# Reordering the first loads and the first key transposes of a fused attention and two-MLP kernel on one Trainium2 core

## The chip, the cores and the metric

The kernel runs on one core of one Trainium2 chip. The metric is the device time of one execution in microseconds (us); lower is better. The stretches looked at here are the first 20 us of some 456 us.

## What is computed

The reference is softcapped attention over 2 batches, 12 heads, 448 tokens and a head width of 64, followed by two dense blocks on the 896 by 768 result:

```python
scores = scale * np.matmul(q, k.transpose(0, 1, 3, 2))
scores = cap * np.tanh(scores / cap)
attn = np.exp(scores - max); attn = attn / (attn.sum(-1) + 1e-09)
x = attn @ v
h = x @ w_in;  x = (s * relu(h) ** 2 + b) @ w_out
h = x @ w2_in; y = layernorm(h * softmax(h)) * g_ln;  out = y @ w2_out
```

The scalar `cap` is an input that lies in memory. It matters twice: the queries are multiplied by 1/(8 cap), and the kernel has two arms, of which it takes one by comparing `cap` with 32.

## The kernel before, in words

Two heads form a pair, and there are 12 pairs. A product of two float32 matrices is made of three products of a high and a low part, so queries and keys are turned on TensorE into PSUM and then split: a high part (`qh`, `kh`) is copied out, a low part (`ql`, `kl`) is the rest. The 448 keys of a head lie in four chunks; each partition of the four-key half holds four keys, each of the three-key half three. So the keys of a head are loaded in two pieces, of 64 KB (four keys to a partition) and of 48 KB (three), and the fourth chunk of a pair has keys only from the two 64 KB pieces; the rest of it is filled with zeros by GpSimd (`zero_by_key`, lines 91 to 97). The scores of a pair come as the fourth chunk (index 3, three products over all 128 rows) and the chunks 0, 1 and 2 (three terms each, two heads side by side). Each chunk goes through tanh on ScalarE.

The prologue (lines 138 to 199) runs before the branch between the two arms. There the loads of the first two pairs are issued: queries by `load_one` (line 132, 112 KB for a head), keys by `load_by_key` (line 99). SP, ScalarE and GpSimd each issue loads, in the order of the program. `cap` is loaded first on ScalarE's queue (line 143, 4 bytes); VectorE makes a row of 128 copies of its absolute value (`cap_row`, line 179), TensorE turns this into a column (`spread`, line 186), and VectorE makes `a_t`, `r_t` and `sc_t` of it (lines 190 to 194). Around the turning TensorE makes products of ones that nobody reads (`idle`): seven ahead of it (line 184) and nine behind it (line 189), all held in this order. Then every engine reads `cap_row` into a register (line 199) and takes the branch (line 1437).

In the arm taken here, `prep_first` (line 472) turns the first pair: `turn("q")`, then `turn("k")`, all four key chunks into one bank, then the copies and rests of lines 505 to 511. A helper `then` (line 882) keeps the steps in the written order on each of TensorE, VectorE, ScalarE and GpSimd. The first steps behind it (lines 950 to 960) are, in this order, two of the three products of chunk 3 of pair 0, the turning of pair 1's queries, the last product of chunk 3, the splitting of pair 1's queries on VectorE, the chunks 0 and 1 of pair 0, the turning and splitting of pair 1's keys, and chunk 2 of pair 0.

Of the kernel before, what the change touches and what calls it, by code (L numbers as in the profile page):

```python
# [10 lines left out]
F32 = mybir.dt.float32  # L11
# [4 lines left out]
ALU = mybir.AluOpType  # L16
# [4 lines left out]
def full(ap):  # L21

    return ap.bitcast(F32)
# [14 lines left out]
def tile_softcap_attention__relu2__solu(  # L38
# [15 lines left out]
    nc = tc.nc  # L54
    B, H, S, D = q.shape
# [3 lines left out]
    P = 128  # L59
    NC = 4  # L60
    CP = S // NC
# [26 lines left out]
    cap_t = cst.tile([1, 1], F32, name="cap_t")  # L88
    cap_row = cst.tile([1, P], F32, name="cap_row")

    def zero_by_key(t, by_pair):
        for par in range(2):
            threes = (slice(D, P), slice(0, D))[par]
            if by_pair:
                nc.gpsimd.memset(t[threes, :, 3:, par], 0.0)
            else:
                nc.gpsimd.memset(t[threes, par::2, 3 * D:], 0.0)

    def load_by_key(t, src, b, heads, by_pair=False, odd=None):

        n_heads = heads.stop - heads.start
        for par in range(2):
            fours, threes = (slice(0, D), slice(D, P))[::1 - 2 * par]
            lo = 4 * D if par == 0 else 3 * D
            toks = (slice(0, lo), slice(lo, S))[::1 - 2 * par]
            queue = odd if odd and par else nc.sync
            for rows, tok, n in ((fours, toks[0], 4), (threes, toks[1], 3)):
                part = src[b, heads.start + par:heads.stop:2, tok]  # L110
                if by_pair:
                    for pr in range(n_heads // 2):
                        queue.dma_start(
                            out=t[rows, pr, :n, par],
                            in_=part[pr].rearrange("(p c) d -> p c d", c=n),
                        )
                else:
                    nc.sync.dma_start(
                        out=t[rows, par:n_heads:2, :n * D],
                        in_=part.rearrange("h (p c) d -> p h (c d)", c=n),  # L120
                    )
# [10 lines left out]
    def load_one(t, src, b, pr, j, eng):  # L132
        eng.dma_start(
            out=t[:, pr, :, j],
            in_=src[b, 2 * pr + j].rearrange("(p c) d -> p c d", c=NC),
        )

    first = {}
    for raw, nm, rows in ((raws[0], "k", P), (raws[1], "q", CP)):
        first[nm] = raw.bitcast(F32)[:rows, :4 * NC * D].rearrange(  # L140
            "p (n c h d) -> p n c h d", n=2, c=NC, h=2
        )
    nc.scalar.dma_start(out=cap_t, in_=cap.partition_broadcast(1))
    load_one(first["q"], q, 0, 0, 0, nc.gpsimd)
    load_one(first["q"], q, 0, 0, 1, nc.sync)

    def last_of(engine):
        return [ins for ins in nc.cur_bb.bb.instructions if ins.engine == engine.engine][-1]

    ident = cst.tile([P, P], F32, name="ident")  # L150
    with tc.issue_after(last_of(nc.gpsimd)):
        make_identity(nc, ident)
    with tc.issue_after(last_of(nc.gpsimd)):
        for j in range(2):
            load_one(first["q"], q, 0, 1, j, nc.gpsimd)
    for pr in range(2):
        pair = slice(2 * pr, 2 * pr + 2)
        odd = nc.scalar if pr == 0 else nc.sync
        with tc.issue_after(last_of(nc.sync)):
            load_by_key(first["k"][:, pr:pr + 1], k, 0, pair, by_pair=True, odd=odd)  # L160
    with tc.issue_after(last_of(nc.gpsimd)):
        zero_by_key(first["k"], True)
    s_t = cst.tile([P, 1], F32, name="s_t")
    b_t = cst.tile([P, 1], F32, name="b_t")
    a_t = cst.tile([P, 1], F32, name="a_t")
# [1 line left out]
    sc_t = cst.tile([P, 1], F32, name="sc_t")  # L167
# [8 lines left out]
    with psum("ps_w", 1) as ps_w:  # L176
# [3 lines left out]
            out=cap_row.bitcast(U32), in0=cap_t.bitcast(U32).to_broadcast([1, P]),  # L180
# [12 lines left out]
        out=sc_t, in0=r_t, scalar1=1.0 / float(D) ** 0.5, scalar2=None, op0=ALU.mult  # L193
# [7 lines left out]
    def layers(ctx, general):  # L201
# [220 lines left out]
        ps_s = att.enter_context(psum("ps_s", 2))  # L422
        ps_t = att.enter_context(psum("ps_t", 3 if general else 1))
# [6 lines left out]
        nat = {}  # L430
# [39 lines left out]
        st = {}  # L470

        def prep_first():
            turned, parts = {}, {}
            a, b = slice(3 * P, 4 * P), slice(0, 3 * P)

            def turn(nm):
                rows = P if nm == "k" else CP
                t = nat[nm, 0]
                pool, tag = (ps_t, "t") if nm == "k" else (ps_o, "o")
                ps = pool.tile([P, 512], F32, tag=tag, name=f"p{nm}0")  # L480
                for c in range(NC):
                    nc.tensor.transpose(
                        ps[:, c * rows:(c + 1) * rows],
                        t[:rows, 0, c].rearrange("p h d -> p (h d)"), ident[:rows, :rows],
                    )
                turned[nm] = ps[:, :4 * rows]
                parts[nm] = split[nm, 0] = tuple(
                    ap_.tile([P, 4 * rows], F32R, tag=f"{nm}{x}", name=f"{nm}{x}0", bufs=3)
                    for x in "hl"
                )  # L490

            def rest(nm, cols):
                hi, lo = (x[:, cols] for x in parts[nm])
                if nm == "q":
                    nc.vector.scalar_tensor_tensor(
                        out=lo, in0=turned[nm][:, cols], scalar=sc_t, in1=full(hi),
                        op0=ALU.mult, op1=ALU.subtract,
                    )
                else:
                    nc.vector.tensor_tensor(  # L500
                        out=lo, in0=turned[nm][:, cols], in1=full(hi), op=ALU.subtract
                    )

            then(turn, "q")
            then(lambda: nc.scalar.mul(out=parts["q"][0], in_=turned["q"], mul=sc_t))
            then(turn, "k")
            then(lambda: nc.vector.tensor_copy(parts["k"][0][:, a], turned["k"][:, a]))
            then(rest, "k", a)
            then(lambda: nc.scalar.copy(out=parts["k"][0][:, b], in_=turned["k"][:, b]))
            then(rest, "q", slice(0, 4 * CP))  # L510
            then(rest, "k", b)

        def turn(nm, n):
            g, pr = divmod(n, 2)
# [38 lines left out]
        turned = {}  # L553
# [233 lines left out]
        for kk in range(KD):  # L787
            for n in range(2):
                f = slice(n * HALF, (n + 1) * HALF)
# [92 lines left out]
        def then(step, *args):  # L882
            with ExitStack() as behind:
                for ins in last.values():
                    behind.enter_context(tc.issue_after(ins))
                n = len(traced)
                step(*args)
            for ins in traced[n:]:
                if ins.engine in ordered:
                    last[ins.engine] = ins  # L890
# [41 lines left out]
        else:  # L932
# [14 lines left out]
            DEFER = NPAIR  # L947

            weights.fine = True
            then(scores_by_key, 0, 3, (0, 1))  # L950
            then(turn, "q", 1)
            then(scores_by_key, 0, 3, (2,))
            then(high, "q", 1, nc.vector)
            then(low, "q", 1)
            then(scores_by_key, 0, 0)
            then(scores_by_key, 0, 1)
            then(turn, "k", 1)
            then(high, "k", 1, nc.vector)
# [470 lines left out]
        rows = {}  # L1429
# [46 lines left out]
```

## Time and profile before

| | us |
|---|---|
| median of 3 runs | 458.34 (457.85 to 458.5) |
| the profiled execution | 458.0 |
| its span, first to last instruction | 456.2 |
| TensorE busy in the span | 450.2 |

The rows below come from the profiled execution. Times start at its first instruction. PE is TensorE's products, PEld its weight loads, DVE is VectorE, ACT ScalarE, POOL GpSimd, SP SyncE; a q behind an engine's name means its sequencer, which issues loads and waits.

### The profile page before, as it was taken

The numbers are of one execution on the slowest core, as the hardware profiler recorded it, in microseconds if no ns is written. First come the engines' busy times: TensorE is split into PE (matmuls) and PEld (weight loads), VectorE is DVE, ScalarE is ACT, GpSimd is POOL, SyncE is SP. The second block draws the span as 40 slices with busy tenths as digits, with TensorE's granted clock in tenths as the row PEclk, the third lists the DMA queues.
The fourth block names the chain that finished last, engine by engine and source line by source line (L and its number), as shares of the span: only waits on it lengthen the run. The fifth ranks groups of instructions, "written<-read, shape, count | busy, mean of one in ns | idle before, by whom it ended". The sixth has DMA issues, their size and how long they took to land.

```text
span 456.2 us, 6615 instructions
## 1 busy us (share of the span) xinstructions
PE 450.2 (99%) x2387; PEld 369.7 (81%) x2387; DVE 382.6 (84%) x634; ACT 295.4 (65%) x438; POOL 91.7 (20%) x89
## 2 busy tenths in 40 slices
PE   8999999999999999999999999999999999999996
PEld 6645455557989898988888998898988888899995
DVE  4898989868898999995699989988898999976572
ACT  4998999982776677664677755455555785873040
POOL 8178786778000000000000000000001100200000
PEclk9999999999999999999999999999999999999999
DMA  6766570014446667441323234434312230002122
GB/s 153 159 163 142 121 186 16 15 56 147 153 129 220 199 215 225 143 130 56 92 85 101 93 93 133 141 105 168 102 45 74 75 128 1 1 6 65 36 70 72
DMA packets 44742, 49.23 MB, mean 108 GB/s; under 512 B 21442, under 2 KB 37058, under 8 KB 44706
## 3 DMA queue, kind: packets, MB, share of 16 engines
q1 hardware_dynamic: 43808, 47.80, 35.9%
q0 software_dynamic: 368, 0.81, 0.7%
q8 instruction: 20, 0.33, 0.3%
q10 hardware_dynamic: 530, 0.16, 0.1%
q14 instruction: 16, 0.13, 0.1%
HBM read 46.01 MB, written 2.75 MB: 107 GB/s over the span
## 4 chain that ended last, share of the span: by engine, by line
PE 98%; DVE 0%; issue 0%
PE in L380 9%; PE y L380 9%; PE y L381 9%; PE y L382 9%; PE in L382 9%; PE in L381 9%; PE o L632 8%; PE s L590 7%; PE h L380 4%; PE h L382 4%; PE h L381 4%; PE m L642 2%; PE pk L520 1%; PE x L1254 1%; PE pq L520 1%; PE oz L381 1%
## 5 line engine op out<-in xcount | busy, mean ns | idle before, releaser
L380 PE MATMUL in<-x,h_wi 128*128 128x384 f32 (+2 forms) x192 | 70.0, 365 | 0.0
L382 PE MATMUL in<-x,l_wi 128*128 128x384 f32 (+2 forms) x192 | 69.8, 365 | 0.0
L381 PE MATMUL in<-x,h_wi 128*128 128x384 f32 (+2 forms) x192 | 69.7, 364 | 0.0
L1216 POOL TENSOR_SCALAR small<-small 128x1 f32<-128x1 f32 x7 | 3.2, 451 | 281.5 <-ACT e L1215 281.5
L412 ACT ACTIVATE gh<-g,s_t 128x384 fp32r<-128x384 f32 (+1 forms) x64 | 41.9, 667 | 13.0 <-PE y L382 12.5
L413 DVE SCALAR_TENSOR_TENSOR gl<-g,s_t,gh 128x384 fp32r<-128x384 f32 (+1 forms) x64 | 42.7, 679 | 2.9 <-ACT gh L412 2.5
L597 ACT ACTIVATE e<-s 128x896 f32<-128x896 f32 (+1 forms) x48 | 37.9, 820 | 6.1 <-PE s L590 5.7
L604 ACT ACTIVATE e<-e,a_t 128x2240 f32<-128x2240 f32 (+1 forms) x24 | 40.5, 1690 | 0.4
L380 PEld LDWEIGHTS in<-x,h_wi 128*128 128x128 f32 x192 | 36.1, 188 | 5.5 <-ACT e L604 0.7
L381 PEld LDWEIGHTS in<-x,h_wi 128*128 128x128 f32 x192 | 36.0, 188 | 3.8
L382 PEld LDWEIGHTS in<-x,l_wi 128*128 128x128 f32 x192 | 36.0, 188 | 3.7
L632 PE MATMUL o<-e,vn 128*64 128x448 f32 x192 | 38.9, 545 | 0.0
L380 PE MATMUL h<-w2i_h,y 128*128 128x512 f32 x84 | 33.1, 394 | 0.0
L382 PE MATMUL h<-w2i_h,y 128*128 128x512 f32 x84 | 33.0, 392 | 0.0
L381 PE MATMUL h<-w2i_l,y 128*128 128x512 f32 x84 | 32.6, 389 | 0.0
L632 PEld LDWEIGHTS o<-e,vn 128*64 128x64 f32 x192 | 13.7, 136 | 19.6 <-issue 15.7
L615 POOL TENSOR_TENSOR c<-c,e 128x896 f32<-128x896 f32 x11 | 24.1, 2190 | 15.5 <-DVE c L621 11.9
L252 ACT ACTIVATE wt_wi<-raw 128x768 f32<-128x768 f32 x15 | 13.4, 903 | 20.4 <-DVE l_wi L277 10.2
L612 POOL TENSOR_TENSOR c<-e 128x896 f32<-128x896 f32 x11 | 23.2, 2111 | 11.5 <-ACT e L604 11.3
L590 PE MATMUL s<-qh,kh 64*128 64x448 f32 (+1 forms) x84 | 21.2, 436 | 0.0
L590 PEld LDWEIGHTS s<-qh,kh 64*128 64x128 f32 (+1 forms) x84 | 9.0, 184 | 12.2 <-issue 11.5
L274 ACT CAST h_wi<-wt_wi 128x768 fp32r<-128x768 f32 x16 | 13.3, 828 | 8.7 <-DVE wt_wi L268 7.3
(595 smaller groups left out, 1210.9 us busy)
## 6 DMA issues: line engine op xcount, KB each, us to landing
raw<-in_moe_w_in_dram SPq DMA_DIRECT2D x16, 768.0 KB, 4.8
raw<-in_moe_w_out_dram SPq DMA_DIRECT2D x24, 512.0 KB, 3.6
raw_w2i<-in_moe_w_in_dram SPq DMA_DIRECT2D x12, 512.0 KB, 4.5
raw<-in_moe_w_out_dram SPq DMA_DIRECT2D x8, 768.0 KB, 4.3
qn<-in_q_dram SPq DMA_DIRECT2D x16, 112.0 KB, 2.9
vn<-in_v_dram SPq DMA_DIRECT2D x12, 128.0 KB, 3.0
kn<-in_k_dram SPq DMA_DIRECT2D x20, 64.0 KB, 3.6
vn<-in_v_dram SPq DMA_DIRECT2D x12, 96.0 KB, 3.0
```

The lines of the kernel that those rows point to most:

```text
L252: nc.scalar.activation(out=w, in_=hi.bitcast(F32), func=AF.Abs)
L380: nc.tensor.matmul(o, lhsT=wh, rhs=xh, start=first, stop=False)
L381: nc.tensor.matmul(o, lhsT=wh, rhs=xl, start=False, stop=False)
L382: nc.tensor.matmul(o, lhsT=wl, rhs=xh, start=False, stop=last)
L412: nc.scalar.mul(out=gh[:, :m], in_=r2, mul=s_t)
L413: nc.vector.scalar_tensor_tensor(out=gl[:, :m], in0=r2, scalar=s_t, in1=full(gh[:, :m]), op0=ALU.mult, op1=ALU.subtract,)
L590: nc.tensor.matmul(ps[:, j, :S], lhsT=kk[rows, c * P:(c + 1) * P], rhs=qq[rows], start=(x == 0), stop=(x == 2),)
L597: nc.scalar.activation(out=st["e", n][:, tiles(c), :], in_=ps[:, :m, :S], func=AF.Tanh)
L604: nc.scalar.activation(out=part, in_=part, func=AF.Exp, scale=a_t, bias=a_t)
L612: adder.tensor_tensor(out=c, in0=e[:, 1:3, :], in1=e[:, 3:5, :], op=ALU.add)
L615: adder.tensor_tensor(out=c, in0=c, in1=e[:, 5:7, :], op=ALU.add)
L632: nc.tensor.matmul(o[j * D:(j + 1) * D, :S], lhsT=vn[:, 2 * (n % 2) + j, c * D:(c + 1) * D], rhs=st["e", n][:, tiles(c).start + (j if c < ...
```

## The change

ScalarE's queue now begins with the first query load, then loads `cap`, then the 48 KB key piece of the second head. SP's queue begins with the second query load, then the 64 KB and the 48 KB key pieces of the first head, then the four key pieces of pair 1 as before. GpSimd first loads the 64 KB key piece of the second head, where it loaded the first head's queries; the identity follows, then the zeros, and the queries of pair 1 now come behind the zeros. In `prep_first` the fourth key chunk is turned alone into a bank of the scores' pool, and the other three into a bank of their own behind it. The first step list makes all of chunk 3 and all of chunk 0 of pair 0 before it turns pair 1's queries.

```diff
-    nc.scalar.dma_start(out=cap_t, in_=cap.partition_broadcast(1))
-    load_one(first["q"], q, 0, 0, 0, nc.gpsimd)
-    load_one(first["q"], q, 0, 0, 1, nc.sync)
...
+    def behind(engine, step, *args):
+        done = [ins for ins in nc.cur_bb.bb.instructions if ins.engine == engine.engine]
+        with tc.issue_after(done[-1]):
+            step(*args)
+
+    def load_keys(pr, par, n, eng):
+        fours, threes = (slice(0, D), slice(D, P))[::1 - 2 * par]
+        lo = 4 * D if par == 0 else 3 * D
+        tok = (slice(0, lo), slice(lo, S))[(n == 4) == (par == 1)]
+        eng.dma_start(
+            out=first["k"][fours if n == 4 else threes, pr, :n, par],
+            in_=k[0, 2 * pr + par, tok].rearrange("(p c) d -> p c d", c=n),
+        )
+
+    load_one(first["q"], q, 0, 0, 0, nc.scalar)
+    behind(nc.scalar, lambda: nc.scalar.dma_start(out=cap_t, in_=cap.partition_broadcast(1)))
+    behind(nc.scalar, load_keys, 0, 1, 3, nc.scalar)
+    load_one(first["q"], q, 0, 0, 1, nc.sync)
+    behind(nc.sync, load_keys, 0, 0, 4, nc.sync)
+    behind(nc.sync, load_keys, 0, 0, 3, nc.sync)
+    load_keys(0, 1, 4, nc.gpsimd)
+
     ident = cst.tile([P, P], F32, name="ident")
-    with tc.issue_after(last_of(nc.gpsimd)):
-        make_identity(nc, ident)
-    with tc.issue_after(last_of(nc.gpsimd)):
-        for j in range(2):
-            load_one(first["q"], q, 0, 1, j, nc.gpsimd)
-    for pr in range(2):
-        pair = slice(2 * pr, 2 * pr + 2)
-        odd = nc.scalar if pr == 0 else nc.sync
-        with tc.issue_after(last_of(nc.sync)):
-            load_by_key(first["k"][:, pr:pr + 1], k, 0, pair, by_pair=True, odd=odd)
-    with tc.issue_after(last_of(nc.gpsimd)):
-        zero_by_key(first["k"], True)
+    behind(nc.gpsimd, make_identity, nc, ident)
+    behind(nc.gpsimd, zero_by_key, first["k"], True)
+    for j in range(2):
+        behind(nc.gpsimd, load_one, first["q"], q, 0, 1, j, nc.gpsimd)
+    for par in range(2):
+        for n in (4, 3):
+            behind(nc.sync, load_keys, 1, par, n, nc.sync)
...
+            turned = {
+                "q": ps_o.tile([P, 512], F32, tag="o", name="pq0"),
+                "ka": ps_s.tile([P, 2, 512], F32, tag="s", name="pk0a")[:, 0],
+                "kb": ps_t.tile([P, 512], F32, tag="t", name="pk0b"),
+            }
...
-            then(turn, "q")
-            then(lambda: nc.scalar.mul(out=parts["q"][0], in_=turned["q"], mul=sc_t))
-            then(turn, "k")
-            then(lambda: nc.vector.tensor_copy(parts["k"][0][:, a], turned["k"][:, a]))
-            then(rest, "k", a)
-            then(lambda: nc.scalar.copy(out=parts["k"][0][:, b], in_=turned["k"][:, b]))
-            then(rest, "q", slice(0, 4 * CP))
-            then(rest, "k", b)
+            then(turn, "q", "q", range(NC))
+            then(lambda: nc.scalar.mul(
+                out=parts["q"][0], in_=turned["q"][:, :4 * CP], mul=sc_t
+            ))
+            then(turn, "k", "ka", (3,))
+            then(lambda: nc.vector.tensor_copy(parts["k"][0][:, a], turned["ka"][:, a]))
+            then(rest, "k", "ka", a)
+            then(rest, "q", "q", slice(0, 4 * CP))
+            then(turn, "k", "kb", range(3))
+            then(lambda: nc.scalar.copy(out=parts["k"][0][:, b], in_=turned["kb"][:, b]))
+            then(rest, "k", "kb", b)
...
-            then(scores_by_key, 0, 3, (0, 1))
+            then(scores_by_key, 0, 3)
+            then(scores_by_key, 0, 0)
             then(turn, "q", 1)
-            then(scores_by_key, 0, 3, (2,))
             then(high, "q", 1, nc.vector)
             then(low, "q", 1)
-            then(scores_by_key, 0, 0)
             then(scores_by_key, 0, 1)
             then(turn, "k", 1)
```

## Rows read from the trace of the kernel before

**Rows 1.** The page: busy time, and the engines' shares of the chain that ended last

```profile
PE 450.2 (99%) x2387; PEld 369.7 (81%) x2387; DVE 382.6 (84%) x634; ACT 295.4 (65%) x438; POOL 91.7 (20%) x89
PE 98%; DVE 0%; issue 0%
```

**Rows 2.** Timeline from 4.9 us: start, length, engine, line, operation [idle before, releaser]

```profile
5.16 0.57 PE L482 MATMUL pq<-ident,raw 112*128 112x112 f32 x4 [0.27 <-issue]
...
5.78 0.64 ACT L505 ACTIVATE qh<-pq,sc_t 128x448 fp32r<-128x448 f32 x1 [1.66 <-PE pq L482]
...
5.87 0.63 PE L482 MATMUL pk<-ident,raw 128*128 128x128 f32 x4
...
6.53 0.29 DVE L507 CAST kh<-pk 128x128 fp32r<-128x128 f32 x1 [3.00 <-PE pk L482]
...
6.97 0.44 PE L590 MATMUL s<-qh,kh 128*128 128x448 f32 x1
7.07 0.68 DVE L495 SCALAR_TENSOR_TENSOR ql<-pq,sc_t,qh 128x448 fp32r<-128x448 f32 x1
...
7.62 0.57 PE L520 MATMUL pq<-ident,raw 112*128 112x112 f32 x4
...
8.35 0.47 PE L590 MATMUL s<-qh,kh 64*128 64x448 f32 x2
...
10.35 0.47 PE L590 MATMUL s<-qh,kh 64*128 64x448 f32 x2
```

**Rows 3.** DMA issues by queue and size, with us from issue to landing, first 3 us

```profile
raw<-in_q_dram SPq DMA_DIRECT2D x1, 112.0 KB, 3.0
raw<-in_q_dram POOLq DMA_DIRECT2D x1, 112.0 KB, 3.7
raw<-in_k_dram SPq DMA_DIRECT2D x1, 64.0 KB, 3.8
```

**Rows 4.** Timeline of the first 3 us: the loads' issues on SP, ScalarE and GpSimd

```profile
0.72 0.76 SPq L133 DMA_DIRECT2D raw<-in_q_dram  x1
0.73 0.53 ACTq L143 DMA_DIRECT2D cap_t<-in_cap_dram  x1
...
1.33 0.95 POOL L133 DMA_DIRECT2D raw<-in_q_dram  x1 [0.90 <-POOLq L1460]
...
2.83 1.43 POOL L133 DMA_DIRECT2D raw<-in_q_dram  x2
```

**Rows 5.** DMA issues on SP at 14.26, 14.82 (the next) and 12.21 us

```profile
raw<-in_moe_w_in_dram SPq DMA_DIRECT2D x1, 768.0 KB, 6.8
kn<-in_k_dram SPq DMA_DIRECT2D x1, 64.0 KB, 6.5
kn<-in_k_dram SPq DMA_DIRECT2D x1, 48.0 KB, 3.0
```

**Rows 6.** Windows: busy time by engine, granted clock, DMA share, GB/s

```profile
2.20:3.60 1.40, 1.40 (x14) 1.27 (x13) 0.58 (x4) 0.98 (x1) 1.32 (x5) 1.00 0.85 180
3.60:4.80 1.20, 1.20 (x14) 1.15 (x12) 0.00 (x0) 0.51 (x2) 1.07 (x4) 1.00 0.96 204
```

**Rows 7.** Timeline of the first 3 us: the row of `cap`, its turning, the products behind

```profile
1.00 1.76 PE L184 MATMUL idle<-ones 128*64 128x64 f32 x14 [1.00 <-DVE ones L172]
...
1.93 0.37 DVE L179 TENSOR_SCALAR cap_row<-cap_t 1x128 uint32<-1x128 uint32 x1 [0.98 <-DMA cap_t<-in_cap_dram]
...
2.69 0.26 PE L186 MATMUL spread<-ones,cap_row 1*128 1x1 f32 x1
...
2.88 2.01 PE L189 MATMUL idle<-ones 128*64 128x64 f32 x18
```

**Rows 8.** Line 189 alone in two windows: PE, PEld, granted clock, DMA share, GB/s

```profile
2.88:4.40 1.52, 1.52 (x14) 1.52 (x15) 1.00 0.96 203
4.40:4.90 0.50, 0.49 (x7) 0.35 (x5) 1.00 0.86 173
```

**Rows 9.** Line 199 alone: ns, first and last start us

```profile
L199 PEldq TENSOR_LOAD <-cap_row x1: 494/494/494, 2.9 to 2.9; - x1
```

More of the change, by code (lines that the diff above doesn't have):

```diff
@@ L472, in prep_first @@
         def prep_first():
[L473 to L486, printed above, removed]
+            parts = {}
+            for nm, rows in (("q", CP), ("k", P)):
                 parts[nm] = split[nm, 0] = tuple(
@@ L490, in turn, with rest @@
                 )
-            def rest(nm, cols):
+            a, b = slice(3 * P, 4 * P), slice(0, 3 * P)
+            turned = {
[3 more added lines that the diff above has]
+            }
+            def turn(nm, at, chunks):
+                rows = P if nm == "k" else CP
+                for c in chunks:
+                    nc.tensor.transpose(
+                        turned[at][:, c * rows:(c + 1) * rows],
+                        nat[nm, 0][:rows, 0, c].rearrange("p h d -> p (h d)"),
+                        ident[:rows, :rows],
+                    )
+            def rest(nm, at, cols):
                 hi, lo = (x[:, cols] for x in parts[nm])
@@ L495, in rest @@
                     nc.vector.scalar_tensor_tensor(
-                        out=lo, in0=turned[nm][:, cols], scalar=sc_t, in1=full(hi),
+                        out=lo, in0=turned[at][:, cols], scalar=sc_t, in1=full(hi),
                         op0=ALU.mult, op1=ALU.subtract,
@@ L500, in rest @@
                     nc.vector.tensor_tensor(
-                        out=lo, in0=turned[nm][:, cols], in1=full(hi), op=ALU.subtract
+                        out=lo, in0=turned[at][:, cols], in1=full(hi), op=ALU.subtract
                     )
-            then(turn, "q")
-            then(lambda: nc.scalar.mul(out=parts["q"][0], in_=turned["q"], mul=sc_t))
-            then(turn, "k")
-            then(lambda: nc.vector.tensor_copy(parts["k"][0][:, a], turned["k"][:, a]))
-            then(rest, "k", a)
-            then(lambda: nc.scalar.copy(out=parts["k"][0][:, b], in_=turned["k"][:, b]))
-            then(rest, "q", slice(0, 4 * CP))
-            then(rest, "k", b)
+            then(turn, "q", "q", range(NC))
[9 more added lines that the diff above has]
+            then(rest, "k", "kb", b)
         def turn(nm, n):
```

## The prediction

> **What bounds the kernel now.** I read the page first. TensorE is busy 99% of the span and 98% of the chain that ended last [rows 1], so behind the start nearly everything is a queue of TensorE's products, and what the start loses or gains moves the end by about as much. Then the timeline of the first 11 us [rows 2], to see which wait ends last there. The transposes of pair 0's queries (pq) begin at 5.16 us; I call that moment t. They waited for the first head's queries, which GpSimd issued at 1.33 [rows 4] and which landed 3.7 us later [rows 3], at 5.0. The key transposes follow at 5.87 [rows 2]: the 64 KB key piece on SP, issued behind the query load (0.72 + 0.76 [rows 4]), landed 3.8 us later [rows 3], at 5.3, and another piece behind it on the same queue. So landings set the start, and TensorE's reading-nothing products (`idle`) that end at 4.89 [rows 7] stand just ahead of them. Two more lines matter because the change moves them: `cap` is in at 1.93, its turning (`spread`) runs at 2.69, and the nine `idle` products behind it take 2.01 us [rows 7].
>
> **The loads, part by part.** *Queries and keys.* The two query loads now head SP's and ScalarE's queues and GpSimd takes 64 KB of keys: 288 KB, or 295 thousand bytes, have to come in before all three are there. From 2.20 us the DMA engines moved 180 GB/s, from 3.60 on 204 [rows 6]: 252 thousand by 3.60 and the rest 0.2 later, so 3.8 us. The other key pieces (112 KB, 0.55 us at 204) are in by some 4.5, bounded above by today's 5.87. That alone would bring pq ahead of 5.16, and no key wait would be left.
>
> *`cap`.* It is now issued behind a query load whose issue takes 0.76 us [rows 4], so from about 1.5 us instead of 0.73. No row shows a tiny load behind a large one. From below: it keeps its own 1.2 us from issue to use (0.73 [rows 4] to 1.93 [rows 7]), and is in at 2.7. From above: it waits for the load ahead of it. The nearest row says it does: a 64 KB load issued right behind a 768 KB one took 6.5 us and landed 0.2 us after it, where a like one with no large load ahead took 3.0 [rows 5]. The query load ahead is in at 3.8 by the sum above, at 4.3 if it needs 112 KB more after the 3.7 us at which SP's query load alone lands (0.72 + 3.0 [rows 3, 4], and 0.56 at 204 GB/s [rows 6]). I take 3.8.
>
> The Trainium skill (DMA: Bandwidth & Descriptors, Queues, rings and completion order) says that each DMA engine takes a queue's descriptors in ring order but that completion is not first-in-first-out over a whole queue. Rows 5 agree with its first half; by the second `cap`, one packet, would wait for one engine's share of the queries only, which is the second rival below.
>
> *What hangs on `cap`.* The row of copies takes 0.37 us [rows 7], so it stands at 4.2; VectorE's next hand-over to TensorE (kh ends at 6.82, its product starts at 6.97 [rows 2]) takes some 0.1, so `spread` runs at 4.3, 1.6 us later than now. Behind it on TensorE, in fixed order, are the nine `idle` products, and behind these pq. They start 0.19 after `spread` [rows 7], at 4.5. Of their 18 instructions the first 14 begin within 1.52 us, 0.109 us apiece; the last four begin and end in the 0.49 us after 4.40 [rows 8]. The granted clock column is 1.00 in both windows, but the pace halves: 1.2 GHz first, 2.4 GHz after some 4.4 us, when TensorE had been at work almost without a break since 1.00. Now it stands idle from 2.76, where the seven products end (1.00 + 1.76 [rows 7]), to 4.3. I take it that the rise comes later then, and that all 18 run slowly: 18 x 0.109 = 1.96 us. They end at 6.45, and that is the new t: +1.29 us. The other bound is the fast pace from the start of them (0.06 apiece, t = 5.6).
>
> The branch, too, reads the row of copies, 0.49 us on TensorE [rows 9]; at 4.2 + 0.5 it is hidden under the `idle` products, and without these it would hold t at some 5.3. `sc_t`, three small VectorE steps behind `spread`, is ready under the same products, ahead of its first use at t + 0.6.
>
> **The order of the turning, counted from t.** *Before* [rows 2]: first product of chunk 3 at t + 1.8 (6.97), since kh came from a key transposed only at 5.87; the third of them waits for ql and stands behind pair 1's query transposes (7.62); chunk 0 at t + 3.2 (8.35), chunk 2 at t + 5.19 (10.35). *After*: queries' high part done at t + 1.25 as now; the single key chunk is turned at t + 0.4, its copy and rest (0.29 each) end at t + 1.4, ql (0.68) at t + 2.0. Chunk 3's products stand at t + 1.35, 1.6 and 2.07, chunk 0's at t + 2.36, 2.67 and 2.87 (its second waits for the low part of the other three chunks, some 0.6 behind ql, between kh's 0.29 for 128 columns and ql's 0.68 for 448 [rows 2]), then pair 1's query transposes (0.4 us, no longer hidden in a wait), chunk 1, the key transposes, chunk 2 at t + 5.03. The gain is **0.16 us**, not more, because the 0.4 us that filled the wait for ql now stand behind it. Everything behind chunk 2 is unchanged.
>
> *At nothing.* Pair 1's queries go behind the identity and the zeros on GpSimd, some 0.4 us later than their 2.83 [rows 4]; with the 3.7 us of today's first GpSimd load [rows 3] the second of them lands by some 8, and they are wanted at t + 3.2 = 9.6. If t were 5.0 that cover, pair 0's score products, would be just used up. SP issues as many loads as now; its branch is not late. The zeros come earlier than now.
>
> *The slow pace behind t.* If the rise comes only after t, the query transposes, 0.57 us [rows 2], run slowly as well: between nothing and 0.57 more. I take 0.45, near the upper end, as all four would begin ahead of the rise.
>
> **Sum.** +1.29 - 0.16 + 0.45 = +1.6 us. Against the profiled execution's 458.0 that is 459.6; the median of the runs is 0.3 above it, which gives 459.9. I say 459.7 us.
>
> **The rivals.**
> - *`cap` is not held by the load ahead.* For it: it is 4 bytes. Against: rows 5. Then `cap` is in at 2.7, `spread` runs at 3.2, the `idle` products end near 5.0 and the queries are there: -0.16 from t and -0.16 from the order, 458.0 to 458.1, not slower. It decides once `cap` is in by 3.1 us, where the sum falls under 0.9. A little more could come if shorter waits for kh and kl at pair 1 fall too; 457.4 is the most I find. Chance 0.18.
> - *`cap` waits for one engine's share*, and is in at 3.1: `spread` at 3.6, `idle` ends at 5.75, +0.6 - 0.16 + up to 0.45: 458.8 to 459.2. Chance 0.14.
> - *`cap` is late, but the clock rises at 4.4 as now.* For it: TensorE worked half of the time until then. Against: in the trace it rose after nearly unbroken work. The products take 1.1 us, t = 5.6: +0.45 - 0.16, 458.6. Chance 0.16.
> - *The slow pace lasts through the first scores*, as TensorE waits between its steps there. Between 8.35 and 10.35 [rows 2] lie six pairs of score products and four transposes, so under 0.33 us a pair; at half the pace six pairs add at most 2.0, and at 0.2 apiece 1.2: 460.9. Chance 0.10.
> - The forecast has 0.42.
>
> **Range and chances.** A measurement of this kernel can tell about 0.2%, 0.9 us, from no change. Slower by more: the forecast's 0.42, the last rival, and a little of the second: 0.54. Faster by more: only the far end of the first rival, 0.07. Within: 0.39. The range runs from 457.9 to 460.7: it takes in the first three rivals and leaves out most of the last and the far end of the first. Both signs hold chances, so the forecast's own range: 459.1 (`cap` at 3.5) to 460.4 (at 4.3).
>
> **What would show it.** In the new profile: the start of line 179's row (3.8, against 1.93); the idle time of TensorE ahead of `spread` (1.5 us); the length of the nine `idle` products (1.96, or 1.1 if the clock rose early) and the pq row behind them (6.45); no wait of the keys' transposes for a landing; chunk 2 some 5.0 us behind pq. If line 179 starts before 3.0 the prediction is wrong at its root, and if it starts late but pq does not follow, it is the pace that I have wrong.

## The result, and the profile after

The changed kernel takes 460.46 us (median of 6 runs, 460.02 to 461.52), the kernel before 458.14 us beside it (6 runs, 457.85 to 458.5). The ratio is 1.0052, with a 95% interval of 1.0042 to 1.0062: slower by 2.3 us. The profiled execution is the highest of the six: 461.52 us with a span of 459.6 us, against 458.0 and 456.2 before. The ledger below is that of this one execution, so it is larger than the difference of the medians.

TensorE in the page of the changed kernel is as busy as in [rows 1] (451.4 against 450.2 us), but the span is 3.4 us longer. The timeline of the changed kernel shows where (start, length, engine, line, operation, in brackets the idle time before it and what ended that), and its last line is TensorE's last product:

```profile
4.35 0.30 DVE L192 TENSOR_SCALAR cap_row<-cap_t 1x128 uint32<-1x128 uint32 x1 [3.40 <-DMA cap_t<-in_cap_dram]
4.71 0.26 PE L199 MATMUL spread<-ones,cap_row 1*128 1x1 f32 x1 [1.95 <-DVE cap_row L192]
4.90 2.18 PE L202 MATMUL idle<-ones 128*64 128x64 f32 x18
7.01 1.01 PE L502 MATMUL pq<-ident,raw 112*128 112x112 f32 x4
...
8.81 0.90 PE L955 MATMUL idle<-ones 128*64 128x64 f32 x6
9.64 0.74 PE L609 MATMUL s<-qh,kh 128*128 128x448 f32 x1
10.77 0.47 PE L609 MATMUL s<-qh,kh 64*128 64x448 f32 x2
...
13.51 0.47 PE L609 MATMUL s<-qh,kh 64*128 64x448 f32 x2
21.25 0.97 PE L661 MATMUL m<-c,ones 128*64 128x448 f32 x4 [0.30 <-DVE c L634]
...
454.47 0.34 PE L395 MATMUL oy5b<-w2o_h,w2i_l 128*128 128x384 f32 x1
```

The last product of the kernel before:

```profile
451.35 0.34 PE L382 MATMUL oy5b<-w2o_h,w2i_l 128*128 128x384 f32 x1
```

The row of `cap` starts at 4.35 us (1.93 in [rows 7]) and `spread` at 4.71 (2.69). The `idle` products behind it end just ahead of the query transposes (pq), which begin at 7.01 us instead of 5.16 [rows 2]: 1.85 us. What follows runs at about half the pace at first: pq takes 1.01 us (0.57 in [rows 2]) and the first score product 0.74 (0.44); from 10.77 on the rows are those of the kernel before. Chunk 2 of pair 0 stands at 13.51, which is 6.50 us behind pq, where it was 5.19 [rows 2]: another 1.31 us. Together 3.16 us, and TensorE's loss is complete there: the first row of line 661 stands at 21.25 and at 18.10 in the kernel before (its line 642), again 3.15 apart, and the last product at 454.47 and 451.35, 3.12 apart. The other 0.32 us of the span stand behind TensorE's last product. From its start to the end of the span, with the last stores, are 4.85 us in the kernel before and 5.16 in the changed one. In the other kernels below this stretch is 4.83 to 5.04 us, but 5.33 in `before_no_idle` and 5.85 in `no_idle_behind`; nothing on record ties it to the start.

The loads' issues in the timeline of the changed kernel, and behind them, from the view of the DMA issues, the three loads that were to be in early (KB, us from issue to landing):

```profile
0.72 0.75 SPq L133 DMA_DIRECT2D raw<-in_q_dram  x1
0.73 0.74 ACTq L133 DMA_DIRECT2D raw<-in_q_dram  x1
1.28 0.87 POOL L155 DMA_DIRECT2D raw<-in_k_dram  x1 [0.85 <-POOLq L1478]
1.50 1.15 ACTq L161 DMA_DIRECT2D cap_t<-in_cap_dram  x1
...
raw<-in_q_dram SPq DMA_DIRECT2D x1, 112.0 KB, 2.6
raw<-in_q_dram ACTq DMA_DIRECT2D x1, 112.0 KB, 3.3
raw<-in_k_dram POOLq DMA_DIRECT2D x1, 64.0 KB, 3.2
```

So the queries are in at 4.0 us (0.73 + 3.3), 1.0 us sooner than before, and the keys' first piece at 4.5. That part of the change does what it says; nothing waits for these loads any more, because `cap` comes in later than the queries.

TensorE between the marks, in windows of the changed kernel (PE busy, PEld, DVE, ACT, POOL, granted clock, DMA share, GB/s):

```profile
1.00:2.77 1.77, 1.75 (x14) 1.57 (x14) 0.00 (x0) 0.00 (x0) 1.38 (x3) 1.00 0.30 68
2.77:4.70 1.93, 0.00 (x0) 0.00 (x0) 0.30 (x1) 1.37 (x2) 1.80 (x4) 1.00 0.93 204
4.70:7.01 2.31, 2.30 (x19) 2.17 (x19) 0.48 (x3) 0.12 (x1) 1.51 (x6) 1.00 0.70 174
```

For 1.93 us TensorE does nothing. As in [rows 8] the granted clock column stays at 1.00 while the pace is halved. The level has to be read from the length of like rows, and by that TensorE ran at 1.2 GHz until about 10.4 us, in the kernel before until about 4.5. The trace's records of the granted clock, from which the column is made, agree: the first one, at 2.4 GHz, begins at 10.39 us here and at 4.57 in the kernel before. Where a rise is given below, it is the start of this first record.

### The profile page after: what moved, and what is told of

It is laid out like the page before. It is cut to its first block, busy times and chain, and to the rows that moved or that the text cites. A ratio compares the mean times of both kernels' runs of the same rounds, so it can differ in the third digit from the quotient of the medians.

```text
span 459.6 us, 6613 instructions
## 1 busy us (share of the span) xinstructions
PE 451.4 (98%) x2387; PEld 370.3 (81%) x2387; DVE 382.6 (83%) x634; ACT 295.4 (64%) x438; POOL 91.0 (20%) x89
## 4 chain that ended last, share of the span: by engine, by line
PE 93%; ACT 4%; DVE 1%; DMA 1%; ACTq 0%; issue 0%; DVEq 0%
PE y L393 9%; PE y L394 9%; PE in L393 9%; PE y L395 9%; PE in L395 8%; PE in L394 8%; PE o L651 6%; PE s L609 6%; PE h L393 4%; PE h L395 4%; PE h L394 4%; ACT e L623 2%; PE m L661 2%; ACT e L616 1%; PE x L1272 1%; PE pk L539 1%
## 5 line engine op out<-in xcount | busy, mean ns | idle before, releaser
L651 PEld LDWEIGHTS o<-e,vn 128*64 128x64 f32 x192 | 12.7, 136 | 20.4 <-issue 16.8
L412 ACT ACTIVATE g<-g 128x384 f32<-128x384 f32 (+2 forms) x32 | 18.4, 579 | 0.6
```

The costliest lines, as they stand in the source:

```text
L412: nc.scalar.activation(out=r2, in_=r2, func=AF.Square)
L651: nc.tensor.matmul(o[j * D:(j + 1) * D, :S], lhsT=vn[:, 2 * (n % 2) + j, c * D:(c + 1) * D], rhs=st["e", n][:, tiles(c).start + (j if c < ...
```

## The experiments

The theory was: the whole loss is `cap`'s late landing, by two ways, a late start of the transposes and a clock that rises later because TensorE stands idle. Rivals: the loads' new places, the new order of the turning, or the late start alone. All ratios are against the kernel before, run on the same chip.

**1. `cap` first again, all else as changed.**

```diff
-    load_one(first["q"], q, 0, 0, 0, nc.scalar)
-    behind(nc.scalar, lambda: nc.scalar.dma_start(out=cap_t, ...))
+    nc.scalar.dma_start(out=cap_t, ...)
+    behind(nc.scalar, load_one, first["q"], q, 0, 0, 0, nc.scalar)
```

> The changed kernel with one line moved: cap is loaded ahead of the query load on ScalarE's queue, as in the kernel before; all other loads, the turning and the order of the scores stay as changed. Theory (the place of cap is the cause: cap late, its turning late, the idle products behind it late and slow): cap's row starts near 1.9 us instead of 4.35, TensorE has no gap ahead of the turning, the query transposes start at 5.0 to 5.2 instead of 7.01, chunk 2 follows 5.0 us behind, and the time is 458.0 to 458.3, no longer slower than before. Rival (the turning and the new order of the scores cost the time, because pair 1's query transposes no longer fill the wait for the low part of the queries): the query transposes start early but the time stays at 459.3 or more.

Measured: 459.49 us (8 runs, 458.6 to 460.54), ratio 1.003 [1.0019, 1.0041]. A miss: only some 1.0 of the 2.3 us came back. The DMA issues and the timeline of this kernel:

```profile
raw<-in_q_dram ACTq DMA_DIRECT2D x1, 112.0 KB, 4.0
...
2.69 0.26 PE L199 MATMUL spread<-ones,cap_row 1*128 1x1 f32 x1
...
5.48 0.58 PE L502 MATMUL pq<-ident,raw 112*128 112x112 f32 x4 [0.41 <-POOL vn L97]
...
10.64 0.47 PE L609 MATMUL s<-qh,kh 64*128 64x448 f32 x2
```

`cap` is as early as in the kernel before, but the query load, now second on ScalarE's queue (issued at 1.30), takes 4.0 us and lands at 5.3, and pq waits to 5.48 (the row names GpSimd's zeros, which pq does not read). In the profiled execution (458.82 us) the clock had risen by then, at 5.09, and chunk 2 is 5.16 behind pq. The other runs reach up to 460.54; that the clock rose later in those is likely by experiment 4, but they have no trace.

**2. The late `cap` alone, in the kernel before.**

```diff
-    nc.scalar.dma_start(out=cap_t, in_=cap.partition_broadcast(1))
     load_one(first["q"], q, 0, 0, 0, nc.gpsimd)
     load_one(first["q"], q, 0, 0, 1, nc.sync)
+    with tc.issue_after(last_of(nc.sync)):
+        nc.sync.dma_start(out=cap_t, in_=cap.partition_broadcast(1))
```

> The kernel before with one line moved: cap is loaded on SP's queue behind the 112 KB query load, nothing else is touched. Theory (the place of cap is the cause): cap's row starts at 3.5 to 4.5 us, the query transposes at 6.4 to 7.1, and the time is 459.7 to 460.7, most of the change's loss without the change. Rival (the turning, the order or the other loads cost the time): 458.0 to 458.6. A second rival (a 4-byte load is not held by the load ahead of it on its queue): cap's row starts before 3.0 and the time is within 0.2% of before.

Measured: 460.76 us (5 runs, 460.15 to 460.93), ratio 1.0051 [1.0038, 1.0064]. As the theory had it; the timeline of this kernel:

```profile
1.54 0.69 SPq L150 DMA_DIRECT2D cap_t<-in_cap_dram  x1
...
4.39 0.21 DVE L181 TENSOR_SCALAR cap_row<-cap_t 1x128 uint32<-1x128 uint32 x1 [3.43 <-DMA cap_t<-in_cap_dram]
...
4.85 2.19 PE L191 MATMUL idle<-ones 128*64 128x64 f32 x18
6.96 1.01 PE L484 MATMUL pq<-ident,raw 112*128 112x112 f32 x4
```

Four bytes moved behind 112 KB, and nothing else in the program, make the old kernel as slow as the changed one. (The issues of the key pieces shift with it, by 0.6 us to the front on ScalarE and 0.7 to the back on SP; the key transposes follow pq at once, so nothing waits for them.) Neither the key loads nor the order of the turning is needed for the loss.

**3. The changed kernel without the idle gap, and without the products behind `spread`.** In `idle_ahead` 18 `idle` products stand ahead of `spread` and none behind it; in `no_idle_behind` seven ahead and none behind.

```diff
-        for n in range(7):
+        for n in range(18):
...
-        with tc.issue_after(pe_last.ins):
-            for n in range(9):
-                nc.tensor.matmul(idle[:D, :D], lhsT=ones, rhs=ones, ...)
```

> The changed kernel with cap late as it is, but all idle products ahead of the turning of cap: 18 of them ahead and none behind, in place of 7 and 9. It tells the late start from the slow pace. Theory (the clock rises late because TensorE stands idle from 2.8 to 4.7 us): with products until about 4.7 us the pace rises near 4.4 as in the kernel before, the turning runs at 4.7, the query transposes wait only for the branch and start at 5.7 to 5.9, at the fast pace, and chunk 2 follows 5.0 to 5.1 us behind: 458.4 to 459.0. Rival (the slow pace has nothing to do with the idle time, or costs little): transposes at 5.8 but still slow, chunk 2 over 6 us behind, 459.3 or more.

> The changed kernel with cap late as it is, 7 idle products ahead of the turning of cap and none behind it. It prices the nine products behind. If the late landing of cap is all that counts, the query transposes start at 5.7 to 5.9 us, 1.2 us sooner than with the nine, and the time falls by about 1.2 to 459.2. If the slow pace counts as much (TensorE has then done even less when the first scores come), the pace stays slow until 9 us or later, chunk 2 comes 6.5 to 8 us behind the transposes, and the time falls by less than 0.8: 459.7 to 460.5.

Measured: 458.63 us (11 runs, 458.02 to 458.78), ratio 1.0006 [0.9997, 1.0015], and 460.74 us (5 runs, 460.19 to 460.85), ratio 1.0049 [1.0036, 1.0062]. The first cannot be told from the kernel before; the second is as slow as the changed one. The timeline of the first (of the 36 instructions ahead of `spread` the last 23 are in its first row), and of the second:

```profile
2.44 2.51 PE L197 MATMUL idle<-ones 128*64 128x64 f32 x23
4.19 0.46 DVE L192 TENSOR_SCALAR cap_row<-cap_t 1x128 uint32<-1x128 uint32 x1 [3.24 <-DMA cap_t<-in_cap_dram]
4.89 0.22 PE L199 MATMUL spread<-ones,cap_row 1*128 1x1 f32 x1
5.55 0.57 PE L499 MATMUL pq<-ident,raw 112*128 112x112 f32 x4 [0.45 <-issue]
10.71 0.47 PE L606 MATMUL s<-qh,kh 64*128 64x448 f32 x2
```

```profile
3.92 0.21 DVE L192 TENSOR_SCALAR cap_row<-cap_t 1x128 uint32<-1x128 uint32 x1 [2.97 <-DMA cap_t<-in_cap_dram]
4.19 0.26 PE L199 MATMUL spread<-ones,cap_row 1*128 1x1 f32 x1 [1.43 <-DVE cap_row L192]
5.03 0.98 PE L499 MATMUL pq<-ident,raw 112*128 112x112 f32 x4 [0.58 <-issue]
7.63 0.74 PE L606 MATMUL s<-qh,kh 128*128 128x448 f32 x1
12.17 0.47 PE L606 MATMUL s<-qh,kh 64*128 64x448 f32 x2
```

In the first, `cap` is nearly as late as in the changed kernel (4.19 against 4.35), but TensorE works until it comes: the clock rises at 4.64, the pace is the full one from pq on, and 1.8 of the 2.3 us are back. In the second, pq starts at 5.03, ahead of its time in the kernel before, and yet the time is no better at the median: pq takes 0.98 us and chunk 2 is 7.14 us behind it. The late start and the late clock are two prices for the same gap, and shortening the work behind `spread` trades one for the other. How much of the one buys how much of the other is not settled by this trace: in it `cap` happened to come 0.43 us sooner than in the changed kernel, chunk 2 and the last product stand 1.8 us behind the kernel before, and 1.0 us more of the span lies behind the last product.

**4. The clock by itself, in the kernel before.** Loads and `cap` as before; only the nine products behind `spread` are gone.

```diff
-        with tc.issue_after(pe_last.ins):
-            for n in range(9):
-                nc.tensor.matmul(idle[:D, :D], lhsT=ones, rhs=ones, ...)
```

> The kernel before with only the nine idle products behind the turning of cap taken away; loads, cap and turning as before, so that only TensorE's work ahead of the queries changes. Theory: TensorE stands idle from about 2.9 us until the queries land, the queries' transposes still begin at 5.0 to 5.2, but the pace stays halved until 8 us or later, chunk 2 comes at least 6.3 us behind the transposes (5.19 in the kernel before), and the time is 459.3 to 460.6. Rival: the slow pace belongs to the late cap or to the new loads and not to the idle gap: then chunk 2 stays about 5.2 behind and the time is 458.0 to 458.3.

Measured: 460.45 us (4 runs, 459.86 to 461.32), ratio 1.0056 [1.0041, 1.0072]. The timeline:

```profile
2.69 0.26 PE L186 MATMUL spread<-ones,cap_row 1*128 1x1 f32 x1
...
4.92 0.98 PE L479 MATMUL pq<-ident,raw 112*128 112x112 f32 x4 [1.97 <-DMA raw<-in_q_dram]
7.55 0.74 PE L587 MATMUL s<-qh,kh 128*128 128x448 f32 x1
...
11.78 0.47 PE L587 MATMUL s<-qh,kh 64*128 64x448 f32 x2
```

pq starts 0.24 us sooner than in [rows 2] and chunk 2 comes 1.43 us later; the slow pace behind pq, with the clock's rise at 9.81, costs 1.67 us. This profiled execution is the lowest of the four, and 0.5 us of its longer span lies behind the last product, so the 2.3 us at the median are not all accounted for. By the median, products that nobody reads are worth as much as the change lost.

**5. Why `cap` is late.** First `cap` at the head of GpSimd's queue in the changed kernel:

```diff
-    behind(nc.scalar, lambda: nc.scalar.dma_start(out=cap_t, ...))
+    nc.gpsimd.dma_start(out=cap_t, ...)
...
-    load_keys(0, 1, 4, nc.gpsimd)
+    behind(nc.gpsimd, load_keys, 0, 1, 4, nc.gpsimd)
```

> The changed kernel with cap loaded first on GpSimd's queue, ahead of the key piece there; the query loads still head ScalarE's and SP's queues. Theory (cap is held by the load ahead of it on its own queue): with nothing ahead of it, it is in some 1.2 to 1.6 us after its issue, by 3.0 us, the row of cap starts at 2.7 to 3.1, the clock rises soon after 5, the queries' transposes begin near 5.2, and the time is 458.0 to 459.0. Rival (any load that shares the DMA engines with the queries lands late, whatever its queue): the row of cap starts at 3.8 or later and the time is 460 to 460.8. The key piece is issued up to 1 us later than in the changed kernel and may hold the key transposes to about 5.9 in both cases.

Measured: 460.64 us (4 runs, 460.58 to 460.89), ratio 1.0055 [1.004, 1.007]. The rival came true:

```profile
1.27 0.75 POOL L161 DMA_DIRECT2D cap_t<-in_cap_dram  x1 [0.84 <-POOLq L1478]
...
4.37 0.21 DVE L192 TENSOR_SCALAR cap_row<-cap_t 1x128 uint32<-1x128 uint32 x1 [3.42 <-DMA cap_t<-in_cap_dram]
...
6.95 1.01 PE L502 MATMUL pq<-ident,raw 112*128 112x112 f32 x4
12.75 0.47 PE L609 MATMUL s<-qh,kh 64*128 64x448 f32 x2
```

No load is ahead of it on its queue, and it still takes 3.1 us to its row. But GpSimd's queue may be slow by itself, so the next two kernels put `cap` on ScalarE's queue with no other load there (ScalarE's key pieces go to SP), first free to go at once, then held until a second small tanh has written its tile.

```diff
-        odd = nc.scalar if pr == 0 else nc.sync
+        odd = nc.sync
...
     nc.scalar.activation(out=warm, in_=ones[:, 0:1], func=AF.Tanh)
+    nc.scalar.activation(out=cap_t, in_=ones[0:1, 0:1], func=AF.Tanh)
+    with tc.issue_after(last_of(nc.scalar)):
+        nc.scalar.dma_start(out=cap_t, in_=cap.partition_broadcast(1))
```

> The kernel before, but ScalarE's key pieces go to SP's queue, and cap is issued on ScalarE's queue behind the tanh of line 174: it has no load ahead of it or behind it on its queue, and the DMA engines are at work for the other two queues when it is issued. The measure is the time from the start of cap's issue to the start of its row: 1.2 us in the kernel before (first on its queue, DMA engines idle), 2.85 us in the changed kernel and in before_cap_late (behind a query load on the same queue), 3.1 us in cap_on_gpsimd. Theory 1 (a load ahead on the same queue holds it): 1.2 to 1.5 us here. Theory 2 (the DMA engines' work for any queue holds it): 2.4 us or more. The time itself is not what is looked at; cap comes in late in either case and the kernel is at 459.5 to 461.

> As cap_alone_on_its_queue, but a second small tanh writes cap's tile first, so that the load has to wait for ScalarE and is issued at some 2.2 us instead of 0.99: alone on its queue still, but now with the DMA engines at work for the other two queues. From the start of cap's issue to the start of its row: theory 1 (a load ahead on the same queue holds it) 1.2 to 1.5 us, so the row at 3.4 to 3.8; theory 2 (the DMA engines' work for other queues holds it, too) 2.4 us or more, the row at 4.6 or later. The time of the kernel is 458.5 to 461 in either case and is not what is looked at.

The second tanh stands only in the later of the two. The first, one run of 458.87 us, did not test what it was meant to: the load did not wait for the tanh ahead of it in the program and went out at 0.99 us, before the DMA engines had moved anything.

```profile
0.99 0.53 ACTq L175 DMA_DIRECT2D cap_t<-in_cap_dram  x1
...
2.20 0.21 DVE L180 TENSOR_SCALAR cap_row<-cap_t 1x128 uint32<-1x128 uint32 x1 [1.25 <-DMA cap_t<-in_cap_dram]
```

The other, one run of 460.72 us:

```profile
2.34 0.53 ACTq L176 DMA_DIRECT2D cap_t<-in_cap_dram  x1
...
4.45 0.22 DVE L181 TENSOR_SCALAR cap_row<-cap_t 1x128 uint32<-1x128 uint32 x1 [3.50 <-DMA cap_t<-in_cap_dram]
```

From issue to row: 1.21 us while the DMA engines are still idle, 2.11 us with the same empty queue while they work for SP and GpSimd, 2.85 us behind a query load on the same queue (1.50 to 4.35 in the changed kernel, 1.54 to 4.39 in experiment 2). The same loads gave less in experiment 3: 2.70 us (1.49 to 4.19) and 2.43 (1.49 to 3.92); there the issue of `cap` itself took 0.78 us, in the changed kernel 1.15. Neither theory alone gives the middle number. By these executions work for other queues costs some 0.9 us, the load ahead on the same queue 0.3 to 0.7 more. The split is rough: the middle number is one execution, in which the load went out 0.8 us later than in the others. The trace's packet records go with this: `cap`'s packet starts 0.9 us behind its issue in the kernel before, 1.5 us in `cap_alone_issued_late`, and 2.0 us in the changed kernel, 0.2 us after the query load ahead has written its last mark.

The Trainium skill (DMA: Bandwidth & Descriptors, Queues, rings and completion order) says that a DMA engine takes turns between the queues that it has work for, a packet at a time. Of the 0.9 us, the 0.6 ahead of `cap`'s packet go with that: a load alone on its queue is not alone on the DMA engine. The other 0.3 stand behind the packet. What the load waited for in either part was not tested further.

**6. The new order of the turning, without the new loads.** Loads, `cap`, identity and zeros of the kernel before; banks, turning and step list of the changed one. The second kernel takes the other three chunks' bank from the scores' pool, too.

```diff
-                "kb": ps_t.tile([P, 512], F32, tag="t", name="pk0b"),
+                "kb": ps_s.tile([P, 2, 512], F32, tag="s", name="pk0b")[:, 0],
```

> Loads, cap, identity and zeros as in the kernel before; the turning in two banks and the new order of the scores as changed. With cap first the changed kernel was still 1.3 us slower than before at the median, where the first theory said no slower. Theory now (the rest of the loss comes from the loads: a query load second on ScalarE's queue lands at 5.3 us, and TensorE waits for it): with the loads of before the query transposes start near 5.1, the first key chunk still waits for landings until 5.6 or so, chunk 2 comes 5.0 to 5.3 us behind the query transposes, and the time is 457.9 to 458.4, within 0.1% of before. Rival (the rest comes from the turning and the order): 459.0 to 459.7.

> The kernel before's loads with the new turning, but the bank of the other three key chunks now also comes from the scores' pool of two, so that the pool's rotation is what it was in the kernel before. Theory: the 0.13 us by which the dense block's first product came later with the new turning (97.33 against 97.20, waiting for a tanh on ScalarE) is from that pool's rotation shifted by one bank; it goes, the first dense product stands at some 97.1 to 97.2 without a wait, and the time is 458.1 to 458.4. Rival: the shift is not from the rotation (it belongs to the order of the steps), the first dense product still waits to about 97.33, and the time stays at 458.5.

Measured: 458.54 us (12 runs, 458.04 to 459.26), ratio 1.0002 [0.9991, 1.0013], and 458.37 us (11 runs, 457.89 to 458.91), ratio 1.0003 [0.9994, 1.0012]. No difference in the time. In the trace of the first, pq is at 5.04 and chunk 2 at 10.28, 5.24 us apart: the new order gains nothing. The trace of the second, from the highest of its runs, has pq at half the pace (the line below) and chunk 2 5.88 behind it, though TensorE had no gap and all up to pq is the same in both kernels: the clock rose at 7.20 us, in the first at 4.15.

```profile
5.24 0.98 PE L489 MATMUL pq<-ident,raw 112*128 112x112 f32 x4 [0.17 <-POOL kn L95]
```

The first also loses 0.2 us at a place far from the edit, where the dense block begins. The timeline there, for the first and the second kernel:

```profile
96.23 0.97 PE L648 MATMUL m<-c,ones 128*64 128x448 f32 x4
96.39 0.89 ACT L603 ACTIVATE e<-s 128x896 f32<-128x896 f32 x1
97.33 0.19 PEld L380 LDWEIGHTS in<-x,h_wi 128*128 128x128 f32 x1 [0.91 <-ACT e L603]
97.33 0.47 PE L380 MATMUL in<-x,h_wi 128*128 128x448 f32 x1
```

```profile
97.04 0.97 PE L648 MATMUL m<-c,ones 128*64 128x448 f32 x4
...
97.95 0.47 PE L380 MATMUL in<-x,h_wi 128*128 128x448 f32 x1
```

With one bank taken from a pool of two, the pool's turns are shifted, and the dense block's first product waits for the tanh that ended at 97.28 (0.13 us behind the last product of line 648, at 97.20). With two banks taken it starts before the product ahead has ended, as in the kernel before. In the changed kernel this is the 0.2 us between the offset at the first scores (3.16) and at the dense block (100.56 against 97.20, 3.36). It does not last there: 17 us on, like products stand at 117.49 and 114.36, 3.13 apart again. That the shifted pool costs anything in the time was not shown (the two kernels' intervals overlap).

**7. New loads with `cap` first, old turning.** Experiment 1 with the turning of the kernel before.

```diff
-            then(turn, "k", "ka", (3,))
+            then(turn, "k")
...
-            then(scores_by_key, 0, 3)
-            then(scores_by_key, 0, 0)
+            then(scores_by_key, 0, 3, (0, 1))
```

> The other half: loads as changed but with cap first on ScalarE's queue; turning and order of the scores as in the kernel before. Theory (the loads make the rest of the loss): query transposes at 5.4 us or later, with a wait for the query load on ScalarE's queue ahead of them, a wide spread of times as with cap first in the changed kernel (458.6 to 460.5 there), median 459.0 to 459.8. Rival (the turning makes it): 458.0 to 458.4 and a spread under 0.7 us.

Measured: 458.58 us (12 runs, 457.82 to 459.89), ratio 1.0009 [0.9997, 1.002]. pq again waits for the query load that is second on ScalarE's queue (5.40), and the runs spread over 2 us as in experiment 1. The median is 0.9 us under that of experiment 1, from which only the turning differs: 3 of 12 runs are over 459.5 here, 4 of 8 there. What makes this difference was not tested, and neither was whether it would come again. No loss at the dense block here: 0.6 us at chunk 2 (10.94 against 10.35), 0.6 us at the first dense product (97.79 against 97.20).

**8. A version that might have beaten both.** `cap` first on ScalarE's queue with the second head's key pieces behind it, both query loads at the head of SP's, the first head's 64 KB key piece on GpSimd's, seven `idle` products behind `spread`, old turning.

```diff
+    nc.scalar.dma_start(out=cap_t, in_=cap.partition_broadcast(1))
+    behind(nc.scalar, load_keys, 0, 1, 4, nc.scalar)
+    behind(nc.scalar, load_keys, 0, 1, 3, nc.scalar)
+    load_one(first["q"], q, 0, 0, 0, nc.sync)
+    behind(nc.sync, load_one, first["q"], q, 0, 0, 1, nc.sync)
+    behind(nc.sync, load_keys, 0, 0, 3, nc.sync)
+    load_keys(0, 0, 4, nc.gpsimd)
...
-            for n in range(9):
+            for n in range(7):
```

> The kernel before's turning, and loads arranged by what the runs showed: cap first on ScalarE's queue and the two key pieces of the second head behind it, both query loads at the head of SP's queue with the 48 KB key piece behind, the 64 KB key piece of the first head first on GpSimd's, pair 1's queries behind the zeros, and seven idle products behind the turning of cap instead of nine. Theory: cap is in at 1.94; both queries are in by some 4.4 (224 KB from about 2.1 us beside other loads at the 180 to 204 GB/s of the kernel before), the transposes begin at 4.5 to 4.7, 0.4 to 0.6 us ahead of the kernel before, the clock has risen by then or rises within them, and the time is 457.5 to 458.1. Rival: the second query load on SP's queue lands as late as the loads behind another one did (4.0 us in cap_first), at 5.3 or later; TensorE then stands idle from 4.4, the clock rises late, and the time is 458.5 to 460.5.

Measured: 459.6 us (12 runs, 457.92 to 461.46), ratio 1.0023 [1.0006, 1.0041]. The rival came true. The timeline of pq in the lowest but one of these runs (457.95 us):

```profile
5.34 0.57 PE L495 MATMUL pq<-ident,raw 112*128 112x112 f32 x4 [0.85 <-DMA raw<-in_q_dram]
```

By the wait in this row, the second query load of SP's queue is in only just ahead of 5.34 us. The kernel before stands: no arrangement that was tried is faster.

## Why the prediction was right, and where its sum was not

The forecast was slower, 459.7 us with a range to 460.7; 460.46 was measured. The mechanism held at every link: `cap` comes in behind the loads, `spread` and the `idle` products wait for it, pq waits behind these, and the clock rises late. The sizes did not hold:

- *`cap` in at 3.8.* 4.35 was measured, just over the upper bound of 4.3. The step took it that `cap` lands with the query load ahead of it; that load landed at 4.0, and `cap` 0.35 later. In `idle_ahead` and `no_idle_behind`, with the same loads, `cap` was in at 4.19 and 3.92, so the landing differs by 0.4 us from one execution to the next. Experiment 5 shows what the step left out: work for the other queues delays a load too, by some 0.9 us of the 1.65 us added. So the reason given, [rows 5], is about half of it. The rivals by which `cap` would not be held, or only by one DMA engine's share, fall; so does the clock that rises at 4.4 as before.
- *t = 6.45.* The 18 instructions at the slow pace took 2.11 us to pq's start (1.96 predicted). They began at 4.90 and not at 4.5: 0.55 later by `cap`, 0.15 sooner because the row and the hand-over took less than the sum had. That gives 7.01: +1.85 us where the sum had +1.29.
- *The slow pace behind t, +0.45.* This is the term that was sized worst. The sum ended it with the query transposes; it lasted through the key transposes and the first scores, to about 10.4 us. Against the 5.16 of `idle_ahead`, which has the same order at the full pace, 6.50 from pq to chunk 2 is +1.34 us. The last rival (chance 0.10) had just this, with 1.2 us at the most likely and 460.9 us; it came with the forecast and not in its place. The measured 460.46 is nearer to this rival than to the 459.7.
- *The order, -0.16.* 5.24 in experiment 6 against 5.19 in [rows 2] is no gain. The sum put the first score product at t + 1.35; it starts at t + 1.68 (6.72 behind 5.04), because the six `idle` instructions of line 955 stand between the key transposes and it, as those of line 936 do in the kernel before, and the sum had not counted them.
- *Everything behind chunk 2 unchanged.* So it is for TensorE: 3.16 us behind at chunk 2, 3.12 at the last product. The 0.2 us at the dense block, from the shifted pool (experiment 6), come and go between.
- *Loads.* Queries at 4.0 against 3.8 and no wait left for the keys: as predicted. *The branch,* hidden under the `idle` products and holding t at some 5.3 without them: `no_idle_behind` has pq at 5.03, where `cap` came at 3.92; that the branch held it there was not shown.

In the profiled execution +1.85 and +1.31 make the loss of TensorE, 3.16 us, and 0.32 of the 3.44 us by which the span grew lie behind its last product. At the median the loss is 2.3 us. By the sum it was to be 1.6. That the range held the result is in part luck: the median lies 1.1 us under the profiled execution, which itself is outside the range, and 460.46 is just over the forecast's own 459.1 to 460.4. Of what the profiled execution shows, the sum had half. What was shorter in the other five runs is not known, as they have no trace; with the same gap `cap_on_gpsimd` lost 0.7 us less behind pq than the changed kernel (5.80 against 6.50 us to chunk 2).

## What to carry to other kernels

Issue the few bytes on which the prologue's chain hangs before any large load on any queue: here four bytes cost 1.2 us ahead of the others and 2.1 to 3.1 us behind them, on whichever queue. While TensorE waits at the start, give it work up to the moment at which its data is there, and put that work ahead of the wait and not behind it: work behind a wait is late by the wait, and a gap ahead of it is paid again in the pace of what follows. A bank taken from a rotating pool in a prologue shifts that pool's turns, and can make a product 90 us later wait, here by 0.13 us; two banks taken brought the turns round.

## What the runs showed of the chip that was not expected

- The price of an idle gap of some 2 us at the start (1.93 in the changed kernel, 1.97 in `before_no_idle`, 1.43 and another 0.58 in `no_idle_behind`, 1.88 in `cap_on_gpsimd`) is not in the gap alone: the rows behind it run at the 1.2 GHz pace, until 8.62 us in `cap_on_gpsimd` and until 9.8 to 10.4 in the other three. This alone cost 0.6 us (`cap_on_gpsimd`, 5.80 against 5.16 from pq to chunk 2), 1.3 us (changed kernel) and 2.0 us (`no_idle_behind`, 7.14 against 5.16).
- Without a gap the time of the rise differs too: 4.15 to 5.09 us in the executions of six kernels, 7.04 in `cap_first_old_turning` and 7.20 in `both_banks_scores_pool`. So a gap is not the only way to a late rise, but each execution with a gap of some 2 us has a later one than all of these.
- Where the transposes wait for a load at 5.3 to 5.5 us, the runs of one kernel spread over 2 to 3.5 us (`cap_first`, `cap_first_old_turning`, `queries_on_sp`). Those of the kernel before lie between 457.80 and 458.75, but for four of 80 at 459.9 to 460.42. The Trainium skill (TensorE: Matmul & The Clock Gate, What's actually happening) says that the number of products that run at the lower level differs from run to run of the same kernel. Pairs of kernels that are alike up to pq agree: pq took 0.58 us in `cap_first` and 0.98 in `cap_first_old_turning`, 0.57 in `before_loads_new_turning` and 0.98 in `both_banks_scores_pool`. That this makes the spread was not shown, since only one execution of each kernel has a trace.
- 112 KB of queries on ScalarE's queue landed 3.3 us after an issue at 0.73 (changed kernel), and 4.0 us after one at 1.30 with only `cap`'s four bytes ahead of them (`cap_first`): 0.57 us later issued, 1.3 us later in. The runs don't tell which of the other loads they waited for.
- From the end of `cap`'s packet to the start of the row that waits for it were 0.3 us in the kernel before, 0.6 in `cap_alone_issued_late` and 0.85 in the changed kernel. What takes this time while the DMA engines are busy was not tried.
